# Attention features: one float32 product per head, on half of TensorE's rows each

## The chip, the cores and the metric

The kernel runs on one core of one Trainium2 chip. The metric is the device time of one execution in microseconds (us). Before the change it is 971.33 us, the median of three runs (971.07 to 971.48).

## What is computed

The input of two MLPs is an attention with random features (FAVOR). For batch 4, 8 heads, 576 tokens and head size 64, with `omega` of 128 x 64:

```python
def phi(x):                                   # x is q or k, scaled by 64 ** -0.25
    proj = np.einsum('bhsd,md->bhsm', x, omega)
    h = proj - np.sum(x * x, axis=-1, keepdims=True) / 2.0
    h = h - np.max(h, axis=-1, keepdims=True)
    return np.exp(h) / np.sqrt(m)
kv = einsum('bhsm,bhsd->bhmd', phi(k), v);  z = sum over s of phi(k)
out = (phi(q) @ kv) / (phi(q) . z + 1e-6)
```

The term in `x * x` is the same for all 128 features of a token, so it falls out when the maximum is taken away, and the kernel leaves it out. The result, 2304 tokens x 512, goes through two MLPs (512 to 2048 to 512), the first with a leaky ReLU whose slopes are `alpha`, the second with a clipped square. All is float32.

## The kernel before

**Attention.** Two heads make a pair: head 0 of a pair stands in partitions 0 to 63 of the q and k tile, head 1 in 64 to 127. There are 16 pairs, four for each batch. `kq` of a pair has 512 columns of k, 512 of q, and a block of 128 columns with the last 64 tokens of k and of q. `features` (line 332) forms the products of blocks of 128 tokens: the block is the stationary operand and `om` (128 x 256) the moving one. `om` holds the scaled omega twice, block-diagonal, so one product gives both heads' features, 2 x 128 columns. Two blocks fill one PSUM bank of 512 columns. VectorE takes the negated maximum of each head and token (line 351), ScalarE the exponentials, 128 columns at a time with that maximum as bias (line 354). Then follow the key sums (line 359), the transposes of the q features (line 414), the quotients (line 450) and `back` (line 473), which writes the attended tokens to `x`.

**Two ways to form a product.** Pairs 0 to 5 (`N_FULL = 6`) use plain float32 products (line 342). For the later pairs, `split_columns` (line 327) makes a float32r part `xh` on ScalarE (line 226) and a rest `xl` on GpSimd or VectorE (line 237 or 236), and `mm3` (line 241) forms the product in three float32r passes with `om_hi` and `om_lo`. The same `mm3` serves the quotients of the later pairs and both MLPs.

**MLPs.** A unit is one slice of 128 hidden features for one group of tokens. Sixteen units make a group's layer; the groups are batch 0, batch 1, batch 2, and batch 3 with the left-over tokens. Weights come as packed 64-bit words and are converted on ScalarE, VectorE and GpSimd (`convert`, line 252), then split into float32r parts `w_hi` and `w_lo` (`split_weights`, line 299).

**Order.** All instructions are put in order by a small planner (`Plan`, line 38) when the program is built. Each piece of work is a stream that asks for engines, tokens or events, and gives an estimated duration for each step. The planner takes the step that can start first; ranks break ties. TensorE's steps of attention have ranks below those of the MLPs, so they go first. On the chip each engine then runs its instructions in that fixed order. Buffers are tokens: there is one token each for the k features, the q features, the left-over features and the transposed features, and two for the q and k tiles (`xs_of_pair`).

**Banks.** PSUM has eight banks. `h0` and `h1` belong to the MLPs' hidden products. Attention may use the other six (`y0` to `y3`, `a0`, `a1`) until the first MLP unit has been projected; from then on `y0` to `y3` go to the MLPs and attention has `a0` and `a1`. `give` (line 321) hands a bank back.

Of the kernel before, what the change touches and what calls it, by code (L numbers as in the profile page):

```python
# [8 lines left out]
F32 = mybir.dt.float32  # L9
# [123 lines left out]
def _dve(n, emit, handicap=0.0):  # L133
    return "dve", 65 + 1.05 * n, emit, handicap
# [18 lines left out]
def _pe(ns, emit):  # L153
    return "pe", ns, emit
# [7 lines left out]
def favor_attention_two_mlps(  # L162
# [21 lines left out]
    P = 128  # L184
# [13 lines left out]
    AHEAD = 5  # L198
    N_FULL = 6
    WARM = 18  # L200

    const = ctx.enter_context(tc.tile_pool(name="const", bufs=1))
    wpool = ctx.enter_context(tc.tile_pool(name="w", bufs=NF))
# [10 lines left out]
    def ev(*key):  # L214
        return events.setdefault(key, Event())

    def done(*key):
        plan.set(ev(*key))

    def bank(tag):  # L220
        return psum.tile([P, 512], F32, tag=tag, name=tag)


    def hi_of(hi, src, dve=None):
        n = src.free_size()
        ops = [_act(n, lambda: nc.scalar.activation(hi, src, AF.Copy))]  # L226
        if dve is not None:
            ops.append(_dve_fast(n, lambda: nc.vector.tensor_copy(hi, src), dve))
        return ops

    def lo_of(lo, src, hi, engines=("dve",), bias=0.0):
        n = src.free_size()
        args = lo, src, hi.bitcast(F32), ALU.subtract
        ops = {
            "dve": _dve(n, lambda: nc.vector.tensor_tensor(*args), bias),  # L235
            "dve2": _dve_two(n, lambda: nc.vector.tensor_tensor(*args), bias),  # L236
            "pool": _pool(n, lambda: nc.gpsimd.tensor_tensor(*args)),  # L237
        }
        return [ops[e] for e in engines]
# [6 lines left out]
    def mm3_ns(n):  # L246
        return 3 * max(109.0, 13.5 + n / 2.4)
# [69 lines left out]
    xs_of_pair, v_slots, split_slot = Tokens([0, 1]), Tokens([0, 1]), Tokens([0])  # L317
    k_slot, q_slot, l_slot, t_slot, den_slot = (Tokens([0]) for _ in range(5))
    kv_slots = Tokens([0, 1])

    def give(tag):
        if tag[0] == "a" or not started:
# [1 line left out]
        else:  # L324
            plan.put(y_banks, tag)

    def split_columns(x, xh, xl, c, key):
        yield hi_of(xh[:, c], x[:, c], 500)
        yield lo_of(xl[:, c], x[:, c], xh[:, c], ("dve2", "pool"), 5000)
        done(*key)  # L330

    def features(pool, xf, xh, xl, t0, n, dst, key, needs):
        yield ev(*needs)
        tag = yield free_banks
        pr = bank(tag)

        def products():
            for t in range(n):
                c = slice((t0 + t) * P, (t0 + t + 1) * P)
                o = pr[:, t * 2 * M : (t + 1) * 2 * M]  # L340
                if xh is None:
                    nc.tensor.matmul(o, xf[:, c], om, start=True, stop=True)  # L342
                else:
                    mm3(o, xh[:, c], xl[:, c], om_hi, om_lo, True, True)

        yield _pe(n * (432 if xh is None else mm3_ns(2 * M)), products)
        pv = pr[:, : 2 * n * M].rearrange("p (n m) -> p n m", m=M)
        nm = pool.tile([P, 4], F32, tag="nm", name="nm", bufs=8)[:, : 2 * n]  # L350
        yield _dve(2 * n * M, lambda: nc.vector.tensor_reduce(nm, pv, AX.X, ALU.max, negate=True))  # L351
        for i in range(2 * n):
            yield _act(
                M, lambda: nc.scalar.activation(dst[:, i, :], pv[:, i, :], AF.Exp, bias=nm[:, i : i + 1]), 40  # L354
            )
        give(tag)
        done(*key)

    def key_sums(pool, kf, lf, vm, vl, pair):
        for key in ("k0", "k1", "l"):  # L360
# [52 lines left out]

    def transposed(qf, lf, qh, ql, h, pair):
        if h < 2:
            yield ev("q0", pair)
            yield ev("q1", pair)
        else:
            yield ev("l", pair)
        tag = yield free_banks  # L420
        ft = bank(tag)

        def products():
            if h < 2:
                for j in range(NJ):
                    nc.tensor.transpose(ft[:, j * P : (j + 1) * P], qf[:, 2 * j + h, :], ident)
            else:
                nc.tensor.transpose(ft[:, :P], lf[:, 1, :], ident)

        yield _pe(109 * (NJ if h < 2 else 1), products)  # L430
        done("qt", pair, h)
        if h < 2:
            src, hi, lo = ft, qh[:, h, :SM], ql[:, h, :SM]
        else:
            src = ft[:, :P].rearrange("m (h t) -> m h t", h=2)
            hi, lo = qh[:, :, SM:], ql[:, :, SM:]
        if pair < N_FULL:
            hi = hi.bitcast(F32)
            n = src.free_size()
            yield [  # L440
                _act(n, lambda: nc.scalar.activation(hi, src, AF.Copy)),
                _dve(n, lambda: nc.vector.tensor_copy(hi, src), 300),
            ]
        else:
            yield hi_of(hi, src)
            yield lo_of(lo, src, hi)
        give(tag)
        done("qs", pair, h)
# [90 lines left out]
    def attend(pool):  # L539
        for pair in range(B * NP):  # L540
            b, hp = divmod(pair, NP)
            r = (3 + b, b - 7)
            yield ev("kq", pair, -1 if pair == 0 else 0)
            yield split_slot
            xt, vm, vl = loaded.pop(pair)
            one = pair < N_FULL
            xh = xl = None
            if not one:
                xh = pool.tile([P, 2 * SM + P], F32R, tag="xh", name="xh")
                xl = pool.tile([P, 2 * SM + P], F32R, tag="xl", name="xl")  # L550
            pieces = [slice(0, SM), slice(2 * SM, 2 * SM + P), slice(SM, 2 * SM)]
            for c, key in zip(pieces, ("xk", "xl", "xq")):
                if one:
                    plan.add(passed(("kq", pair, -1 if key == "xk" and pair == 0 else 0), (key, pair)), *r)
                else:
                    plan.add(split_columns(xt, xh, xl, c, (key, pair)), *r)
            yield k_slot
            kf = pool.tile([P, NJ * 2, M], F32, tag="kf", name="kf")
            plan.add(features(pool, xt, xh, xl, 0, 2, kf[:, :4], ("k0", pair), ("xk", pair)), *r)
            plan.add(features(pool, xt, xh, xl, 2, 2, kf[:, 4:], ("k1", pair), ("xk", pair)), *r)  # L560
            yield l_slot
            lf = pool.tile([P, 2, M], F32, tag="lf", name="lf")
            plan.add(features(pool, xt, xh, xl, 2 * NJ, 1, lf, ("l", pair), ("xl", pair)), *r)
            yield q_slot
            qf = pool.tile([P, NJ * 2, M], F32, tag="qf", name="qf")
            plan.add(features(pool, xt, xh, xl, NJ, 2, qf[:, :4], ("q0", pair), ("xq", pair)), *r)
            plan.add(features(pool, xt, xh, xl, NJ + 2, 2, qf[:, 4:], ("q1", pair), ("xq", pair)), *r)
            plan.add(reload(pool, pair, ("k0", "k1", "l", "q0", "q1") if one else ("xk", "xl", "xq")), *r)
            yield ev("v", pair)
            plan.add(key_sums(pool, kf, lf, vm, vl, pair), *r)  # L570
            yield t_slot
            qh = pool.tile([M, 2, S], F32R, tag="qh", name="qh")
            ql = pool.tile([M, 2, S], F32R, tag="ql", name="ql")
            for h in range(3):
                plan.add(transposed(qf, lf, qh, ql, h, pair), *r)
            plan.add(back(pool, qh, ql, b, hp, pair), *r)
            plan.add(hand_back(pair), *r)
            for key in ("k0", "k1", "l", "q0", "q1"):
                yield ev(key, pair)
            plan.put(split_slot, 0)  # L580

    def reload(pool, pair, keys):
# [2 lines left out]
        plan.put(xs_of_pair, 0)  # L585
        if pair + 2 < B * NP:
            yield from load_pair(pool, pair + 2)

    def passed(key, to):
        yield ev(*key)  # L590
        done(*to)

    def hand_back(pair):
        yield ev("qt", pair, 2)
# [196 lines left out]
    ident = const.tile([P, P], F32, name="ident")  # L791
    alpha_sb = const.tile([P, NF], F32, name="alpha_sb")
    half = const.tile([P, 1], F32, name="half")
    om_hi = const.tile([P, 2 * M], F32R, name="om_hi")
    om_lo = const.tile([P, 2 * M], F32R, name="om_lo")

    ctx.enter_context(tc.manual_schedule())
    att = ExitStack()
# [2 lines left out]
    om = pool.tile([P, 2 * M], F32, name="om")  # L801
    nc.vector.memset(om, 0.0)
    nc.vector.memset(half, 0.5)
    nc.vector.memset(om_lo.bitcast(F32), 0.0)

    warm = const.tile([P, 1], F32, name="warm")
    nc.scalar.activation(warm, half, AF.Exp)
    w = bank("h0")
    for i in range(WARM):
        nc.tensor.matmul(w[:, : 2 * M], om_lo[:, :M], om_lo, start=i == 0, stop=i == WARM - 1)  # L810
    for i in range(2):
        nc.scalar.dma_start(om[i * D : (i + 1) * D, i * M : (i + 1) * M], omega)
    vts = []
# [23 lines left out]
    def constants():  # L837
        make_identity(nc, ident)
        nc.scalar.activation(om, om, AF.Copy, scale=QK_SCALE)
        nc.scalar.activation(om_hi, om, AF.Copy)  # L840
        nc.vector.tensor_tensor(om_lo, om, om_hi.bitcast(F32), ALU.subtract)

    def setup():
        yield "act", 500, constants

    plan.add(setup(), 0)
    plan.add(load(alpha_sb, alpha, ("alpha",)), 0)
# [60 lines left out]
```

## Time and profile before

| | |
|---|---|
| median of the runs | 971.33 us |
| profiled execution, its own time | 974.34 us |
| its span | 972.5 us |
| TensorE products busy | 944.9 us |
| VectorE, ScalarE, GpSimd busy | 566.4, 530.7, 480.6 us |
| mean granted TensorE clock | 0.99 |
| first MLP product starts | 59.5 us |
| last attention x is written | about 300 us |

The profile is of one execution, and its span is the time from its first to its last instruction. PE is TensorE's products, PEld its weight loads, DVE is VectorE, ACT is ScalarE, POOL is GpSimd, SP the engine that issues most DMAs. Groups are named out<-in by the program's tiles. The end of a TensorE record is modelled, and records overlap, so the distance between two starts is the better measure of what one costs. The granted clock is 1.00 at 2.4 GHz and 0.50 at 1.2 GHz.

### The profile page before, as it was taken

The page shows a single profiled execution, that of the slowest core. Times are in us where ns is not written, and L with a number is a line of the kernel's source. Part 1 is how long each engine was busy: PE and PEld are TensorE (multiplying, and loading weights), DVE is VectorE, ACT ScalarE, POOL GpSimd, SP SyncE. Part 2 cuts the span into 40 slices and gives each one's busy share as a digit, 9 for nine tenths or more (in the row PEclk, how much of TensorE's full clock was granted, in tenths as well). Part 3 has the DMA queues.
Part 4 walks back from the last instruction along what each step waited for, and adds up shares of the span by engine and source line. Part 5 has one row for each costly group of instructions (what it writes and reads, how often), then busy time and mean ns, then how long its engine had stood idle before and what let it go on. Part 6 is the DMA issues. An engine that isn't in the chain of part 4 may idle for free.

```text
span 972.5 us, 13293 instructions
## 1 busy us (share of the span) xinstructions
PE 944.9 (97%) x4742; PEld 795.9 (82%) x4742; DVE 566.4 (58%) x949; ACT 530.7 (55%) x1131; POOL 480.6 (49%) x403
## 2 busy tenths in 40 slices
PE   8999989899999999999999999999999999999997
PEld 7877877778888888888888888888887888888886
DVE  4898778678666786556763443354336333534442
ACT  6978777677665565345442354455445444544443
POOL 0545766576445868546663334444443444333320
PEclk9999999799999999999999999999999999999999
DMA  6544444331200322202310000001001000100002
GB/s 181 151 141 136 126 133 142 107 120 38 78 1 2 107 75 99 65 1 87 130 66 1 1 1 1 0 1 44 1 1 43 1 1 1 44 1 1 1 1 65
DMA packets 33858, 53.35 MB, mean 55 GB/s; under 512 B 20993, under 2 KB 21121, under 8 KB 33793
## 3 DMA queue, kind: packets, MB, share of 16 engines
q1 hardware_dynamic: 33632, 52.45, 17.1%
q8 instruction: 37, 0.61, 0.3%
q14 instruction: 29, 0.23, 0.1%
q10 hardware_dynamic: 160, 0.07, 0.0%
HBM read 47.78 MB, written 4.72 MB: 54 GB/s over the span
## 4 chain that ended last, share of the span: by engine, by line
PE 86%; DVE 8%; ACT 3%; issue 1%; POOL 1%; DMA 1%; ACTq 0%; POOLq 0%; DVEq 0%
PE h L244 13%; PE h L242 13%; PE h L243 13%; PE y L244 11%; PE y L242 11%; PE y L243 11%; PE a L242 3%; PE a L244 3%; PE a L243 3%; PE a L377 2%; PE y L342 1%; DVE x_lo L236 1%; ACT kf L354 1%; DVE den L465 1%; DVE nm L351 1%
## 5 line engine op out<-in xcount | busy, mean ns | idle before, releaser
L237 POOL TENSOR_TENSOR w_lo<-w,w_hi 128x512 fp32r<-128x512 f32 x256 | 334.1, 1307 | 381.7 <-ACT w_hi L226 375.0
L226 ACT ACTIVATE w_hi<-w 128x512 fp32r<-128x512 f32 x256 | 161.3, 632 | 220.3 <-PE h L243 155.0
L242 PE MATMUL h<-x_hi,w_hi 128*128 128x512 f32 (+1 forms) x640 | 239.5, 374 | 1.4 <-ACT w_hi L226 1.3
L244 PE MATMUL h<-x_hi,w_lo 128*128 128x512 f32 (+1 forms) x640 | 237.4, 371 | 1.6 <-POOL w_lo L237 1.6
L243 PE MATMUL h<-x_lo,w_hi 128*128 128x512 f32 (+1 forms) x640 | 236.9, 370 | 0.0
L244 PEld LDWEIGHTS h<-x_hi,w_lo 128*128 128x128 f32 x640 | 121.2, 189 | 23.5 <-POOL w_lo L237 2.9
L242 PEld LDWEIGHTS h<-x_hi,w_hi 128*128 128x128 f32 x640 | 121.6, 190 | 21.4 <-ACT w_hi L226 1.5
L243 PEld LDWEIGHTS h<-x_lo,w_hi 128*128 128x128 f32 x640 | 121.5, 190 | 19.1
L226 ACT ACTIVATE g_hi<-h 128x512 fp32r<-128x512 f32 (+1 forms) x160 | 88.7, 554 | 85.7 <-DVE h L656 46.7
L235 DVE TENSOR_TENSOR g_lo<-h,g_hi 128x512 fp32r<-128x512 f32 (+1 forms) x160 | 100.3, 635 | 53.1 <-ACT g_hi L226 50.4
L654 DVE TENSOR_SCALAR t<-h 128x512 f32<-128x512 f32 x80 | 51.0, 638 | 135.4 <-PE h L244 133.7
L269 POOL TENSOR_TENSOR w<-w,raw 128x512 uint32<-128x512 uint32 x64 | 86.2, 1348 | 48.3 <-DVE w L268 26.0
L242 PE MATMUL y<-g_hi,w_hi 128*128 128x512 f32 x256 | 101.3, 396 | 1.2 <-ACT kf L354 1.2
L244 PE MATMUL y<-w_hi,g_lo 128*128 128x512 f32 x256 | 100.2, 391 | 2.3 <-DVE g_lo L235 2.3
L243 PE MATMUL y<-g_lo,w_hi 128*128 128x512 f32 x256 | 100.2, 391 | 0.3 <-DVE g_lo L235 0.3
L650 DVE TENSOR_SCALAR t<-h,alpha_sb 128x512 f32<-128x512 f32 x80 | 55.6, 695 | 76.5 <-PE h L244 74.9
L242 PE MATMUL y<-w_hi,g_hi 128*128 128x512 f32 x256 | 100.1, 391 | 0.0
L243 PE MATMUL y<-w_lo,g_hi 128*128 128x512 f32 x256 | 100.0, 391 | 0.0
L244 PE MATMUL y<-g_hi,w_lo 128*128 128x512 f32 x256 | 100.0, 390 | 0.0
L655 ACT ACTIVATE t<-t,half 128x512 f32<-128x512 f32 x80 | 54.4, 680 | 62.4 <-DVE t L654 62.4
L656 DVE TENSOR_TENSOR h<-h,t 128x512 f32<-128x512 f32 x80 | 51.5, 644 | 49.7 <-ACT t L655 49.7
L272 DVE SCALAR_TENSOR_TENSOR w<-raw,w 128x512 uint32<-128x512 uint32 x64 | 55.8, 887 | 14.6 <-POOL w L269 14.5
(129 smaller groups left out, 1442.3 us busy)
## 6 DMA issues: line engine op xcount, KB each, us to landing
raw<-w SPq DMA_DIRECT2D x64, 512.0 KB, 3.9
kq<-kq SPq DMA_DIRECT2D x15, 576.0 KB, 3.8
vm<-v SPq DMA_DIRECT2D x16, 256.0 KB, 3.2
out<-x SPq DMA_DIRECT2D x16, 256.0 KB, 2.0
vl<-v SPq DMA_DIRECT2D x32, 16.0 KB, 2.9
out<-x SPq DMA_DIRECT2D x4, 128.0 KB, 2.3
kq<-kq SPq DMA_DIRECT2D x1, 320.0 KB, 3.3
kq<-kq SPq DMA_DIRECT2D x1, 256.0 KB, 2.9
```

The costliest lines, as they stand in the source:

```text
L226: ops = [_act(n, lambda: nc.scalar.activation(hi, src, AF.Copy))]
L235: "dve": _dve(n, lambda: nc.vector.tensor_tensor(*args), bias),
L237: "pool": _pool(n, lambda: nc.gpsimd.tensor_tensor(*args)),
L242: nc.tensor.matmul(out_, wh, mh, start=first, stop=False)
L243: nc.tensor.matmul(out_, wh, ml, start=False, stop=False)
L244: nc.tensor.matmul(out_, wl, mh, start=False, stop=last)
L269: yield _pool(n, lambda: nc.gpsimd.tensor_tensor(d, d, low, ALU.add))
L272: lambda: nc.vector.scalar_tensor_tensor(d, e, 0x80000000, d, ALU.bitwise_and, ALU.bitwise_or),
L650: yield _dve(n, lambda: nc.vector.tensor_scalar(tn, hn, 0.0, a, ALU.min, ALU.mult))
L654: yield _dve(n, lambda: nc.vector.tensor_scalar(tn, hn, -1.0, 1.0, ALU.max, ALU.min))
L655: yield _act(n, lambda: nc.scalar.activation(tn, tn, AF.Square, bias=half[:, 0:1], scale=0.5), 50)
L656: yield _dve(n, lambda: nc.vector.tensor_tensor(hn, hn, tn, ALU.max))
```

## The change

All 16 pairs now form the features of their 512 k and 512 q tokens in the same way. For each block of 128 tokens and each head there is one float32 product of 64 rows: the block's 64 partitions of that head, times the head's 64 x 128 piece of `om`. The products of head 0 go to one bank and those of head 1 to another, four blocks of 128 columns in each, and the exponentials of each head are a stream of their own. `features` takes both banks before it starts, and the new token `two_banks` lets only one `features` gather banks at a time. The block of left-over tokens keeps a full product of 128 rows, in float32 for all pairs. The float32r parts of q, k and omega are gone, with `split_columns` and `passed`. The transposes of a head wait for that head's features. The q and k tile of every pair is handed back when its features are done. Setup's planned duration falls from 500 to 300 ns, and the warm-up products use a zeroed tile of their own.

```diff
+    ROWS_NS = 264
+    two_banks = Tokens([0])
-    def split_columns(x, xh, xl, c, key):
-        yield hi_of(xh[:, c], x[:, c], 500)
-        yield lo_of(xl[:, c], x[:, c], xh[:, c], ("dve2", "pool"), 5000)
-        done(*key)
-    def features(pool, xf, xh, xl, t0, n, dst, key, needs):
...
+    def exponentials(pool, pr, tag, dst, key):
+        n = dst.shape[1]
+        pv = pr[:, : n * M].rearrange("p (n m) -> p n m", m=M)
+        nm = pool.tile([P, 4], F32, tag="nm", name="nm", bufs=8)[:, :n]
+        yield _dve(n * M, lambda: nc.vector.tensor_reduce(nm, pv, AX.X, ALU.max, negate=True))
+        for i in range(n):
+            yield _act(
+                M, lambda: nc.scalar.activation(dst[:, i, :], pv[:, i, :], AF.Exp, bias=nm[:, i : i + 1]), 40
+            )
         give(tag)
         done(*key)
+    def features(pool, x, t0, f, keys, needs, r):
+        yield ev(*needs)
+        yield two_banks
+        tags = []
+        for h in range(2):
+            tags.append((yield free_banks))
+        plan.put(two_banks, 0)
+        prs = [bank(tag) for tag in tags]
+        def products():
+            for t in range(NJ):
+                c = slice((t0 + t) * P, (t0 + t + 1) * P)
+                for h in range(2):
+                    rows = slice(h * D, (h + 1) * D)
+                    o = prs[h][:, t * M : (t + 1) * M]
+                    nc.tensor.matmul(o, x[rows, c], om[rows, h * M : (h + 1) * M], start=True, stop=True)
+        yield _pe(NJ * ROWS_NS, products)
+        for h in range(2):
+            plan.add(exponentials(pool, prs[h], tags[h], f[:, h::2, :], keys[h]), *r)
+    def last_features(pool, x, lf, key, needs):
+        yield ev(*needs)
+        tag = yield free_banks
+        pr = bank(tag)
+        o = pr[:, : 2 * M]
+        yield _pe(
+            432, lambda: nc.tensor.matmul(o, x[:, 2 * NJ * P : 2 * NJ * P + P], om, start=True, stop=True)
+        )
+        yield from exponentials(pool, pr, tag, lf, key)
...
     def transposed(qf, lf, qh, ql, h, pair):
         if h < 2:
-            yield ev("q0", pair)
-            yield ev("q1", pair)
+            yield ev(f"q{h}", pair)
...
-            plan.add(features(pool, xt, xh, xl, 0, 2, kf[:, :4], ("k0", pair), ("xk", pair)), *r)
-            plan.add(features(pool, xt, xh, xl, 2, 2, kf[:, 4:], ("k1", pair), ("xk", pair)), *r)
+            plan.add(features(pool, xt, 0, kf, keys, ("kq", pair, -1 if pair == 0 else 0), r), *r)
...
-            plan.add(reload(pool, pair, ("k0", "k1", "l", "q0", "q1") if one else ("xk", "xl", "xq")), *r)
+            plan.add(reload(pool, pair, ("k0", "k1", "l", "q0", "q1")), *r)
...
     def constants():
         make_identity(nc, ident)
         nc.scalar.activation(om, om, AF.Copy, scale=QK_SCALE)
-        nc.scalar.activation(om_hi, om, AF.Copy)
-        nc.vector.tensor_tensor(om_lo, om, om_hi.bitcast(F32), ALU.subtract)
     def setup():
-        yield "act", 500, constants
+        yield "act", 300, constants
```

## Rows read from the trace of the kernel before

**Rows 1.** The page: busy time, share of the span and instructions of each engine.

```profile
span 972.5 us, 13293 instructions
PE 944.9 (97%) x4742; PEld 795.9 (82%) x4742; DVE 566.4 (58%) x949; ACT 530.7 (55%) x1131; POOL 480.6 (49%) x403
```

**Rows 2.** The page: the chain that ended last, shares of the span by engine.

```profile
PE 86%; DVE 8%; ACT 3%; issue 1%; POOL 1%; DMA 1%; ACTq 0%; POOLq 0%; DVEq 0%
```

**Rows 3.** Stages: stretch, its length, each engine's busy time (records), clock, DMA share, GB/s.

```profile
20.00:59.50 39.50, 36.82 (x214) 30.87 (x212) 35.08 (x67) 37.11 (x117) 18.34 (x17) 1.00 0.54 158
59.50:110.00 50.50, 47.59 (x280) 39.90 (x279) 45.09 (x87) 38.02 (x111) 29.63 (x27) 1.00 0.38 116
110.00:239.00 129.00, 116.99 (x633) 97.10 (x632) 100.33 (x186) 94.02 (x233) 86.30 (x73) 0.95 0.37 117
239.00:300.00 61.00, 61.00 (x353) 52.59 (x352) 39.46 (x78) 37.44 (x103) 28.38 (x26) 1.00 0.10 32
```

**Rows 4.** TensorE's waits, 59.5 to 239 us: total us, times, longest us.

```profile
PE a L242 <- ACT kf L354: 2.8, 3, 2.0
PE h L244 <- POOL w_lo L237: 1.6, 3, 0.7
PE a L242 <- ACT lf L354: 1.4, 1, 1.4
PE h L242 <- ACT w_hi L226: 1.3, 1, 1.3
```

**Rows 5.** Stages of 6 us, columns as in rows 3.

```profile
176.00:182.00 6.00, 2.92 (x13) 2.43 (x13) 4.27 (x9) 3.20 (x10) 4.36 (x4) 0.67 0.49 174
182.00:188.00 6.00, 5.92 (x21) 5.34 (x22) 2.31 (x4) 4.09 (x11) 3.36 (x4) 0.50 0.41 132
```

**Rows 6.** TensorE in order of time, first stage: start us, us, instruction, records.

```profile
13.07 1.90 PE L377 MATMUL y<-vm,kf 128*128 128x65 f32 x16
14.80 1.04 PE L426 MATMUL y<-ident,qf 128*128 128x128 f32 x8
...
17.84 1.89 PE L342 MATMUL y<-om,kq 128*128 128x256 f32 x8
19.57 0.65 PE L456 MATMUL y<-qh,kv_hi 128*128 128x288 f32 x2
```

**Rows 7.** Groups by line: records, busy us, mean ns, idle before and releaser.

```profile
L237 POOL TENSOR_TENSOR xl<-kq,xh 128x512 fp32r<-128x512 f32 x20 | 26.0, 1300 | 11.6 <-ACT xh L226 11.6
L342 PE MATMUL y<-om,kq 128*128 128x256 f32 x82 | 21.5, 410 | 0.9 <-ACT om L839 0.9
L226 ACT ACTIVATE xh<-kq 128x512 fp32r<-128x512 f32 x20 | 12.5, 624 | 0.0
L342 PE MATMUL a<-om,kq 128*128 128x256 f32 x26 | 6.9, 379 | 0.0
L237 POOL TENSOR_TENSOR xl<-kq,xh 128x128 fp32r<-128x128 f32 x10 | 5.2, 523 | 0.3 <-ACT xh L226 0.3
L226 ACT ACTIVATE xh<-kq 128x128 fp32r<-128x128 f32 x10 | 3.0, 302 | 0.0
```

**Rows 8.** TensorE in order of time: two MLP passes, then feature passes.

```profile
68.23 0.40 PE L243 MATMUL h<-x_lo,w_hi 128*128 128x512 f32 x1
68.47 0.40 PE L244 MATMUL h<-x_hi,w_lo 128*128 128x512 f32 x1
...
68.83 0.28 PE L243 MATMUL y<-om_lo,xh 128*128 128x256 f32 x1
68.95 0.29 PE L244 MATMUL y<-om_hi,xl 128*128 128x256 f32 x1
```

**Rows 9.** TensorE in order of time: one product behind float32 key sums, one behind float32r.

```profile
91.62 0.38 PE L242 MATMUL a<-qh,kv_hi 128*128 128x288 f32 x1
...
94.15 0.30 PE L242 MATMUL a<-qh,kv_hi 128*128 128x288 f32 x1
```

**Rows 10.** TensorE in order of time: a feature product that waited for its bank.

```profile
182.08 0.58 PE L242 MATMUL a<-om_hi,xh 128*128 128x256 f32 x1 [1.96 <-ACT kf L354]
```

**Rows 11.** DMA issues: records, KB each, median us from issue to landing.

```profile
kq<-kq SPq DMA_DIRECT2D x15, 576.0 KB, 3.8
```

More of the change, by code (lines that the diff above doesn't have):

```diff
@@ L325, in give @@
             plan.put(y_banks, tag)
-    def split_columns(x, xh, xl, c, key):
-        yield hi_of(xh[:, c], x[:, c], 500)
-        yield lo_of(xl[:, c], x[:, c], xh[:, c], ("dve2", "pool"), 5000)
-        done(*key)
-    def features(pool, xf, xh, xl, t0, n, dst, key, needs):
[L333 to L352, printed above, removed]
+    def exponentials(pool, pr, tag, dst, key):
[4 more added lines that the diff above has]
+        for i in range(n):
             yield _act(
@@ L545, in attend @@
             xt, vm, vl = loaded.pop(pair)
[L546 to L556, printed above, removed]
+            kq_in = ("kq", pair, 0)
             yield k_slot
             kf = pool.tile([P, NJ * 2, M], F32, tag="kf", name="kf")
-            plan.add(features(pool, xt, xh, xl, 0, 2, kf[:, :4], ("k0", pair), ("xk", pair)), *r)
-            plan.add(features(pool, xt, xh, xl, 2, 2, kf[:, 4:], ("k1", pair), ("xk", pair)), *r)
+            keys = ("k0", pair), ("k1", pair)
+            plan.add(features(pool, xt, 0, kf, keys, ("kq", pair, -1 if pair == 0 else 0), r), *r)
             yield l_slot
             lf = pool.tile([P, 2, M], F32, tag="lf", name="lf")
-            plan.add(features(pool, xt, xh, xl, 2 * NJ, 1, lf, ("l", pair), ("xl", pair)), *r)
+            plan.add(last_features(pool, xt, lf, ("l", pair), kq_in), *r)
             yield q_slot
             qf = pool.tile([P, NJ * 2, M], F32, tag="qf", name="qf")
-            plan.add(features(pool, xt, xh, xl, NJ, 2, qf[:, :4], ("q0", pair), ("xq", pair)), *r)
-            plan.add(features(pool, xt, xh, xl, NJ + 2, 2, qf[:, 4:], ("q1", pair), ("xq", pair)), *r)
-            plan.add(reload(pool, pair, ("k0", "k1", "l", "q0", "q1") if one else ("xk", "xl", "xq")), *r)
+            plan.add(features(pool, xt, NJ, qf, (("q0", pair), ("q1", pair)), kq_in, r), *r)
+            plan.add(reload(pool, pair, ("k0", "k1", "l", "q0", "q1")), *r)
             yield ev("v", pair)
@@ L587, in reload @@
             yield from load_pair(pool, pair + 2)
-    def passed(key, to):
-        yield ev(*key)
-        done(*to)
     def hand_back(pair):
@@ L793, in favor_attention_two_mlps @@
     half = const.tile([P, 1], F32, name="half")
-    om_hi = const.tile([P, 2 * M], F32R, name="om_hi")
-    om_lo = const.tile([P, 2 * M], F32R, name="om_lo")
     ctx.enter_context(tc.manual_schedule())
@@ L803, in favor_attention_two_mlps @@
     nc.vector.memset(half, 0.5)
-    nc.vector.memset(om_lo.bitcast(F32), 0.0)
     warm = const.tile([P, 1], F32, name="warm")
     nc.scalar.activation(warm, half, AF.Exp)
+    warm_w = const.tile([P, 2 * M], F32R, name="warm_w")
+    nc.vector.memset(warm_w.bitcast(F32), 0.0)
     w = bank("h0")
     for i in range(WARM):
-        nc.tensor.matmul(w[:, : 2 * M], om_lo[:, :M], om_lo, start=i == 0, stop=i == WARM - 1)
+        nc.tensor.matmul(w[:, : 2 * M], warm_w[:, :M], warm_w, start=i == 0, stop=i == WARM - 1)
     for i in range(2):
```

## The prediction

> **What bounds the kernel now.** I read the busy times first [rows 1]: TensorE is busy for 97% of the span and no other engine for more than 58%. The chain of work that ended last agrees: 86% of it is TensorE [rows 2]. So an instruction taken off TensorE is worth its own duration, wherever TensorE is the engine that the others wait for. Whether it is has to be read stage by stage [rows 3]. From 20 to 59.5 us, before the first MLP product, only attention runs, and two engines are full: TensorE 36.8 and ScalarE 37.1 of 39.5 us. From 59.5 to 239 us attention and the first MLP group share TensorE; it fills 94% of the part up to 110 us and 91% of the rest, and no other engine is over 90%. From 239 to 300 us TensorE is full, and after 300 us no attention is left, so the change touches nothing there. The waits of TensorE between 59.5 and 239 us are short ones: a product for a PSUM bank that ScalarE empties, and an MLP product for a weight part [rows 4]. One such wait has a second price: from 176 to 188 us the mean granted clock is 0.67 and then 0.50, the 1.2 GHz level in place of 2.4, after TensorE had been busy for only 2.9 of 6 us; the two rows together give up about 5 us [rows 5].
>
> **The change, part by part.** The unit is one block of 128 tokens of one pair: k and q have four blocks each, and one shared block holds the left-over tokens. A pair has 8 + 1 blocks, 16 pairs have 128 + 16.
>
> *What a block costs before.* In pairs 0 to 5 a float32 product leaves two records; eight records take from 17.84 to 19.57 us, 216 ns each, so a block costs 432 ns [rows 6]. That makes 54 products and 108 records, which the groups show [rows 7]. In pairs 6 to 15 a block is three float32r passes that start 0.12 us apart, 360 ns [rows 8].
>
> *What a block costs after.* Two products of half the rows and half the columns leave four records. By proportion, a record of 128 columns streams in 216 / 2 = 108 ns. A weight load is no faster: the 65-column products of the key sums, with little to stream, still take 1.73 us for 16 records, 108 ns each [rows 6]. No row of before shows two products on different row halves, so there are two ends. If both halves stream and load side by side, a block takes 2 x 108 = 216 ns. If one record follows the other, it takes 4 x 108 = 432 ns, which is today's price. I take the side-by-side end with a start cost on each record: the 256-column float32r pass takes 120 ns, 12 ns over the 108 of one load [rows 6, 8], and 216 + 4 x 12 = 264 ns. The plan's new constant says the same number, which I don't count as evidence.
>
> The Trainium skill (TensorE: Matmul & The Clock Gate, "Measured speedup vs the span model") gives 3.07 times for four row tiles. Scaled to two tiles that is 1.53 times, an estimate of 282 ns for a block, and the sum below would be 9.4 us in place of 11.3.
>
> *Pairs 0 to 5.* 48 blocks x (432 - 264) = 8.1 us less TensorE work, nearly all of it before 59.5 us. There ScalarE is as full as TensorE: it has 39.5 - 37.1 = 2.4 us of free time from 20 us on [rows 3], and the exponentials stay as they are. Some of ScalarE's work in the stage (weight conversions, exponentials of pairs 4 and 5) can give way. The ends are 0 and 8.1; I take half, 4.0 us. ScalarE is what is late next.
>
> *Pairs 6 to 15.* 80 blocks x (360 - 264) = 7.7 us less. The left-over block stays at full height and is float32 now: 10 x (432 - 360) = 0.7 us more. Net 7.0 us, beside MLP work that fills TensorE at once, so I count all of it.
>
> *Kinds of product side by side.* The features of pairs 6 to 15 were float32r amid float32r MLP products; they are float32 now. A float32r product right behind a float32 one shows 0.38 us in place of 0.30 [rows 9], 0.08 us. Three groups a pair (k, q, left-over) make 30 such changes: 2.4 us if each pays and none does already, 0 if the planner puts them beside the float32 key sums and transposes. I take 1.2 us of loss.
>
> *Splits removed.* ScalarE loses 12.5 + 3.0 = 15.5 us and GpSimd 26.0 + 5.2 = 31.2 us, all in pairs 6 to 15 [rows 7]. Neither is the bound. What it can give TensorE is its waits for weight parts, 1.6 + 1.3 = 2.9 us [rows 4], because a 1.3 us split no longer stands ahead of them in GpSimd's order. Between 0 and 2.9 I take 1.5 us of gain. A pair's k products also no longer wait for their own split; attention stays ahead of the MLP groups that use it, so I count nothing.
>
> *Two banks at once.* One group of products now asks for two banks, and two is all that attention has while the MLPs run. Behind the waiting product in TensorE's order stand MLP products, and all else waits for those. Before, five product groups of a pair each asked for one bank; after, two ask for two and one for one. The nearest row is a k product that waited 1.96 us for ScalarE's exponentials [rows 10]; such waits on kf and lf sum to 4.2 us over nine pairs before [rows 4]. The ends are 4.2 us of gain, if fewer requests mean fewer waits, and a 1.96 us wait for each of the 20 groups, 39 us of loss; by the sum in the rows I take 0.
>
> *At no cost.* The scaled omega's two float32r parts go from the start, but the first product waits for omega itself only. Each head's transposes wait for that head's features alone, which is earlier. The k and q tile is held until its features are done and not just its splits, so the load for the pair after next starts some microseconds later; it lands in 3.8 us [rows 11], against a pair's period of some 24 us (ten pairs in the 240 us after 59.5). With that cover gone it would cost up to 3.8 us a pair.
>
> *Sum.* 4.0 + 7.0 - 1.2 + 1.5 + 0 = 11.3 us. The profiled execution took 974.3 us (its span 972.5 and 1.8 around it) and becomes 963.0. The median of the runs is 971.3, 3.0 lower, so the forecast is **960.0 us**.
>
> **The rivals.**
> *R1, loads one after another (slower).* Four half-height loads of 108 ns follow each other and a block costs 432 ns. For it: the key sums show a load as a floor that no short stream gets below [rows 6], and a block doubles its loads from two to four. Against it: today's loads already run beside a stream, and the halves share no rows. Pairs 0 to 5 then gain nothing, pairs 6 to 15 lose 80 x 72 ns + 0.7 = 6.5 us, changes of kind 1.2, and the relief of 1.5 is the only gain: 6.2 us, 977.5 us. It decides once a block costs over about 370 ns, where 128 blocks give back what they save. The Trainium skill (TensorE: Matmul & The Clock Gate, "LDWEIGHTS (loading the stationary operand)") says that load time goes by columns and not by rows, which is this rival's premise; TensorEngine Tiling (Array Packing), "Key Properties", says that different tiles may load and multiply in parallel, which is against it. No row here shows either.
>
> *R2, each change between full and half height empties the array.* A 512-column record lasts 0.40 us while the next starts after 0.24 [rows 8]; if that tail of 0.16 us must run out whenever the height changes, 32 groups, in and out, cost 64 x 0.16 = 10.2 us and leave 1.1 of 11.3: 970.2 us. Nothing in the rows of before excludes it, since all its products have full height. The Trainium skill (TensorEngine Tiling, "Key Properties") says that a change of tiling mode drains TensorE, without a figure.
>
> *R3, the pair of banks brings new waits.* If ten of the 20 late k and q groups wait for 1 us longer than today, 10 us of the 11.3 go: 970.0 us; a further stretch like that at 176 us [rows 5] would make it 975.
>
> *R4, all is delivered.* Blocks at 216 ns and a ScalarE that gives way in full: 48 x 216 = 10.4, 80 x 144 - 0.7 = 10.8, relief 2.9, no loss at changes: 24.1 us, 947.2 us.
>
> **How the numbers follow.** Forecast 0.48, R1 0.13, R2 0.10, R3 0.09, R4 0.20. A measurement of this kernel can tell 0.2%, 1.9 us. Faster: the forecast, R4, and 0.08 of R2 and R3 together, 0.76. Within 0.2%: 0.08, from R2 and R3. Slower: R1 and 0.03 of R2 and R3, 0.16. The forecast's own range is 953 to 966 us (block 216 to 282 ns, first stage 1 to 8 us). The range with the rivals goes from R4's 946 to 974, which leaves R1 out.
>
> **What would show it.** Starts of four records of a block spanning about 264 ns show the block's price; 216 is R4, 432 is R1. A gap of 0.16 us before and after each group of 16 such records is R2. The first MLP product, at 59.5 us now, should come 3 to 5 us earlier, and ScalarE should be the fuller engine of that stage. Waits of TensorE for ScalarE's exponentials should stay near 4 us in sum before the first group ends; 10 us more is R3. The first MLP group should end some 11 us earlier than at about 239 us, and after 300 us the stretch up to the end should be as long as it is. A block over 370 ns, or TensorE's waits grown by more than what its products save, makes the forecast wrong.

## The result, and the profile after

The kernel after takes 954.68 us in the median (954.25 to 956.27), the kernel before 971.2. The ratio is 0.9836 with a 95% interval of 0.9819 to 0.9853: 16.5 us faster, where 11.3 was forecast. The profiled execution took 956.27 us, against 974.34 before; these two lie 18.1 us apart, so the stages below add up to more than the 16.5 us of the medians.

The page of the kernel after: span, busy times, and the chain that ended last. Its rows answer to [rows 1, 2].

```profile
span 954.4 us, 13551 instructions
PE 931.8 (98%) x4908; PEld 776.5 (81%) x4908; DVE 557.9 (58%) x944; ACT 515.8 (54%) x1102; POOL 453.6 (48%) x375
PE 88%; DVE 6%; ACT 4%; issue 1%; DMA 0%; POOL 0%; ACTq 0%; DVEq 0%; POOLq 0%
```

TensorE is still the bound. To see where the time went, the span is cut at two events: the first MLP product, and the end of the second MLP group (its last unit's copy to `x` begins). Stages of the kernel before, then of the kernel after; columns as in rows 3.

```profile
6.50:59.50 53.00, 50.26 (x278) 42.55 (x278) 41.28 (x77) 46.41 (x152) 18.99 (x18) 1.00 0.56 162
59.50:349.00 289.50, 274.25 (x1475) 229.61 (x1474) 221.09 (x401) 198.32 (x495) 178.25 (x153) 0.98 0.28 88
349.00:972.00 623.00, 616.15 (x2975) 519.79 (x2973) 303.49 (x470) 284.11 (x484) 281.74 (x219) 1.00 0.09 29
```

```profile
6.50:58.40 51.90, 45.03 (x374) 35.27 (x374) 37.84 (x78) 44.70 (x145) 18.54 (x18) 0.97 0.55 164
58.40:331.10 272.70, 266.51 (x1547) 217.54 (x1546) 205.01 (x381) 177.93 (x459) 139.44 (x117) 0.99 0.26 85
331.10:954.00 622.90, 615.91 (x2974) 519.63 (x2972) 314.47 (x484) 291.26 (x498) 294.07 (x226) 1.00 0.09 33
```

The stage before the MLPs gives 1.1 us, the middle stage 16.8, the rest nothing. In the middle stage TensorE's unfilled time falls from 289.5 - 274.25 = 15.3 us to 272.7 - 266.51 = 6.2, and the mean clock goes from 0.98 to 0.99. So about 9 us of the 16.8 are idle time that went, and some 3 to 5 us are time at the 1.2 GHz level (an estimate from the rows; part of the slow time was idle too). Before, two stretches ran at the lower clock, the one in [rows 5] and one at 134 us; after, one at 162 us is left. First the kernel before, then the kernel after:

```profile
134.00:140.00 6.00, 4.02 (x16) 3.01 (x15) 3.58 (x6) 4.80 (x14) 3.96 (x3) 0.75 0.52 170
162.00:166.20 4.20, 4.15 (x21) 3.45 (x22) 3.63 (x5) 2.76 (x7) 2.68 (x3) 0.59 0.46 162
```

Little is left for the products themselves. The waits point the same way: those that the profile lists in this part sum to 14.5 us before and 6.2 after. Besides [rows 4] the kernel before has these, and two of 0.8 and 0.7 us for exponentials.

```profile
PE a L426 <- DVE num L468: 1.3, 2, 1.0
PE y L242 <- ACT kf L354: 1.2, 1, 1.2
PE a L426 <- DVE ql L235: 1.2, 1, 1.2
PE a L428 <- DVE ql L235: 1.1, 1, 1.1
PE a L242 <- DVE ql L235: 1.1, 2, 0.9
```

TensorE's longest waits in the kernel after, 59 to 235 us; they answer to [rows 4]. Three more sum to 1.3 us.

```profile
PE a L361 <- ACT kf L339: 1.8, 1, 1.8
PE a L243 <- ACT lf L339: 1.3, 1, 1.3
PE a L373 <- DVE kv_lo L424: 1.0, 1, 1.0
PE h L245 <- POOL w_lo L238: 0.8, 1, 0.8
```

What a group of half-height products costs, amid MLP products (TensorE in order of time, kernel after). L361 is the new product; a bank is called y or a, its number left out.

```profile
183.23 0.39 PE L244 MATMUL h<-x_lo,w_hi 128*128 128x512 f32 x1
183.46 0.39 PE L245 MATMUL h<-x_hi,w_lo 128*128 128x512 f32 x1
183.78 1.16 PE L361 MATMUL a<-om,kq 64*128 64x128 f32 x16
184.87 0.50 PE L243 MATMUL y<-g_hi,w_hi 128*128 128x512 f32 x1
185.21 0.39 PE L244 MATMUL y<-g_lo,w_hi 128*128 128x512 f32 x1
```

And one group record by record, where the two banks have different names (kernel after, behind transposes).

```profile
66.81 0.37 PE L361 MATMUL y<-om,kq 64*128 64x128 f32 x1
66.81 0.37 PE L361 MATMUL a<-om,kq 64*128 64x128 f32 x1
67.02 0.27 PE L361 MATMUL y<-om,kq 64*128 64x128 f32 x1
67.03 0.27 PE L361 MATMUL a<-om,kq 64*128 64x128 f32 x1
67.13 0.27 PE L361 MATMUL y<-om,kq 64*128 64x128 f32 x1
67.14 0.27 PE L361 MATMUL a<-om,kq 64*128 64x128 f32 x1
...
67.69 0.27 PE L361 MATMUL y<-om,kq 64*128 64x128 f32 x1
67.70 0.27 PE L361 MATMUL a<-om,kq 64*128 64x128 f32 x1
67.90 0.70 PE L373 MATMUL a<-om,kq 128*128 128x256 f32 x2
```

The two heads' records start within 0.01 us of each other, and the next two 0.11 us later: the halves run fully side by side, and a block costs two steps, some 0.22 us. But the first step takes 0.21 us, the last 0.20. In the MLP rows a group lasts 183.78 to 184.87, 1.09 us. The record ahead takes 0.32 us to the next start and the one behind 0.34, where 0.23 is usual. A group costs 1.09 + 0.09 + 0.11 = 1.29 us, and a quarter of it is 322 ns a block; 8 steps of 0.112 would be 0.90. Going to half height and back thus costs 0.4 us a group.

### The profile page after: what moved, and what is told of

The parts are those of the page before. It is cut to its first block, busy times and chain, and to the rows that moved or that the text cites. A ratio compares the mean times of both kernels' runs of the same rounds, so it can differ in the third digit from the quotient of the medians.

```text
span 954.4 us, 13551 instructions
## 1 busy us (share of the span) xinstructions
PE 931.8 (98%) x4908; PEld 776.5 (81%) x4908; DVE 557.9 (58%) x944; ACT 515.8 (54%) x1102; POOL 453.6 (48%) x375
## 4 chain that ended last, share of the span: by engine, by line
PE 88%; DVE 6%; ACT 4%; issue 1%; DMA 0%; POOL 0%; ACTq 0%; DVEq 0%; POOLq 0%
PE h L243 13%; PE h L245 13%; PE h L244 13%; PE y L243 12%; PE y L245 12%; PE y L244 12%; PE a L243 2%; PE a L361 2%; PE a L245 2%; PE a L244 2%; PE a L395 2%; DVE nm L336 1%; PE a L443 1%; ACT kf L339 1%; DVE x_lo L237 1%
## 5 line engine op out<-in xcount | busy, mean ns | idle before, releaser
L273 DVE SCALAR_TENSOR_TENSOR w<-raw,w 128x512 uint32<-128x512 uint32 x64 | 59.0, 928 | 8.8 <-POOL w L270 8.7
```

Source lines behind the costliest of these rows:

```text
L273: lambda: nc.vector.scalar_tensor_tensor(d, e, 0x80000000, d, ALU.bitwise_and, ALU.bitwise_or),
```

## The experiments

Theory W: the gain is less product time on TensorE. Theory S: most of it is shorter waits and less time at 1.2 GHz, because the splits of q and k are gone from ScalarE and GpSimd. Theory O: it came with the new order that the planner made. Times are medians beside runs of the kernel before on the same chip (971.0 to 971.3 us).

**full32**: splits dropped, full-height products for all pairs, on the kernel before.

```diff
-            one = pair < N_FULL
+            one = True
             xh = xl = None
```

> The kernel before with the splits of q and k dropped and nothing else: all 16 pairs use full-height float32 blocks at 432 ns. TensorE gets 80 x 72 ns + 0.7 = 6.5 us more product work. Theory W (the gain of the change is product time alone): 971.2 + 6.5 = 977.7 us. Theory S (some 10 us of the gain are shorter waits and less time at 1.2 GHz, because ScalarE and GpSimd no longer split q and k): 977.7 - 10 = 967 to 969 us. Theory O (these 10 us came with the new order of instructions, whatever it was): anything from 966 to 985 us, with TensorE's waits from 59 to 340 us not tied to the splits.

Measured 962.88 us, ratio 0.991 (0.9889 to 0.9931). By the estimate TensorE has 6.5 us more product work, and the kernel is 8.1 us faster: dropping the splits is worth some 14.6 us. W falls. S has the direction, but its 967 to 969 us is missed by 4 us, and O's range is missed too.

**idle_splits**: the reverse, on the kernel after.

```diff
+            if pair >= N_FULL:
+                for c in (slice(0, SM), slice(2 * SM, 2 * SM + P), slice(SM, 2 * SM)):
+                    plan.add(idle_split(xt, xh, xl, c), *r)   # hi_of, lo_of as before
```

> The kernel after, with the splits of q and k of pairs 6 to 15 put back on ScalarE and GpSimd as they were; nothing reads their results. TensorE's products stay as in the kernel after. Theory S: the waits and the 1.2 GHz time come back, 963 to 966 us. Theory W: 954 to 957 us. Theory O: either, since the order changes again.

968.94 us, ratio 0.9986 (0.9968 to 1.0004): 14.3 us slower than after, with the same products, and 3 us slower than theory S said. Two experiments from either side give nearly the same price.

**idle_scalar, idle_gpsimd**: one engine's half of them each. The cut is against idle_splits; each run has one of the two new lines.

```diff
-        yield hi_of(xh[:, c], x[:, c], 500)
-        yield lo_of(xl[:, c], x[:, c], xh[:, c], ("dve2", "pool"), 5000)
+        yield hi_of(xh[:, c], x[:, c])                        # idle_scalar
+        yield lo_of(xl[:, c], x[:, c], x[:, c], ("pool",))    # idle_gpsimd
```

> The kernel after with only the ScalarE half of the splits of pairs 6 to 15 put back (15.5 us of work that nothing reads). If ScalarE's load makes the 14 us that both halves cost together: 966 to 970 us. If GpSimd's makes it: 954 to 957 us. If they share it: 959 to 963 us.

> The kernel after with only the GpSimd half of the splits of pairs 6 to 15 put back (31.2 us of work that nothing reads, without a wait for ScalarE). If GpSimd's load makes the 14 us: 966 to 970 us. If ScalarE's makes it: 954 to 957 us. If they share it: 959 to 963 us.

959.08 us (0.9858 to 0.9887) with ScalarE's half and 968.76 us (0.9953 to 0.9987) with GpSimd's. GpSimd's half alone brings all 14 us, with 25.4 us of GpSimd's time by its trace and not the 31.2 expected; ScalarE's half brings 4.4. The two don't add up.

**same_order_gpsimd**: work for GpSimd that the planner does not see.

```diff
+            if idle is not None:                              # in products(), pairs 6 to 15
+                c = slice(t0 * P, (t0 + NJ) * P)
+                nc.gpsimd.tensor_tensor(idle[:, c], x[:, c], x[:, c], ALU.subtract)
```

> The kernel after with 20 subtractions of 128 x 512 put on GpSimd, one behind each k and q group of pairs 6 to 15 (26 us, nothing reads them). The planner does not know of them, so every other instruction of every engine keeps the order of the kernel after. If GpSimd's time itself is what TensorE waits for: 962 to 969 us, as with idle_gpsimd. If idle_gpsimd was slow because the planner made another order: 954 to 957 us.

958.49 us, ratio 0.986 (0.9831 to 0.9889): 3.8 us slower than after, between the two answers. With 21.9 us of GpSimd's work back by the trace (25.4 in idle_gpsimd) and all else in its order, about a quarter of the 14 us returns; the interval overlaps that of the kernel after, so this 3.8 is rough. The other 10 us were seen only where the planner had the splits to place. In the plan a GpSimd step also keeps VectorE's `dve2` steps from starting, since both ask for `ports` (`USES` in `Plan`), so planned splits move VectorE's work too. No run takes that apart.

The order-kept part has a visible side on VectorE. Two groups of its weight conversion over the whole span, in the kernel after and then in this run:

```profile
L273 DVE SCALAR_TENSOR_TENSOR w<-raw,w 128x512 uint32<-128x512 uint32 x64 | 59.0, 928 | 8.8 <-POOL w L270 8.7
L269 DVE TENSOR_SCALAR w<-raw 128x512 uint32<-128x512 uint32 x64 | 38.1, 599 | 0.6 <-ACT raw L265 0.6
```

```profile
L273 DVE SCALAR_TENSOR_TENSOR w<-raw,w 128x512 uint32<-128x512 uint32 x64 | 61.4, 965 | 10.1 <-POOL w L270 9.8
L269 DVE TENSOR_SCALAR w<-raw 128x512 uint32<-128x512 uint32 x64 | 40.0, 629 | 0.7 <-ACT raw L265 0.7
```

Together they are busy 4.3 us longer, while the maxima that VectorE reads from PSUM (`nm`, 128 x 4 from bank a) take 683 and 682 ns. How much of the 3.8 us comes by this was not measured.

**after_latency230, before_latency230**: the same work in another order.

```diff
-    LATENCY = {"pe": 210.0, "dma": 2200.0}
+    LATENCY = {"pe": 230.0, "dma": 2200.0}
```

> The kernel after with the planner's latency behind TensorE at 230 ns in place of 210: the same instructions in another order. Theory S: 952 to 958 us, as after. Theory O (a new order alone moves the time by 10 us): outside of 948 to 962 us.

> The kernel before with the planner's latency behind TensorE at 230 ns in place of 210: the same instructions in another order. Theory S: 968 to 975 us, as before. Theory O: outside of 964 to 978 us, or as low as 958 us if the order before was an unlucky one.

955.72 us (0.9806 to 0.9865) and 967.52 us (0.9941 to 0.999): +1.0 and -3.5 us. The expectation for the second (968 to 975) missed by half a microsecond. In these two draws an order alone moves 1 and 3.5 us, and the order before was perhaps somewhat unlucky; neither draw crosses the gap.

The middle stages of these kernels, from first MLP product to end of second group (columns as in rows 3).

full32:

```profile
59.30:338.00 278.70, 273.50 (x1385) 227.94 (x1384) 217.88 (x389) 188.31 (x479) 151.12 (x123) 1.00 0.29 95
```

idle_splits:

```profile
58.30:345.40 287.10, 274.51 (x1546) 222.93 (x1545) 213.09 (x383) 190.62 (x487) 171.96 (x150) 0.97 0.25 81
```

idle_gpsimd:

```profile
58.00:342.90 284.90, 273.12 (x1546) 219.66 (x1545) 212.27 (x382) 181.38 (x463) 166.46 (x148) 0.98 0.26 82
```

idle_scalar:

```profile
57.90:331.40 273.50, 265.95 (x1545) 216.32 (x1544) 206.74 (x377) 189.20 (x483) 138.38 (x115) 1.00 0.26 85
```

same_order_gpsimd:

```profile
58.50:334.70 276.20, 268.75 (x1547) 218.50 (x1546) 210.28 (x381) 178.41 (x459) 161.22 (x137) 0.99 0.26 84
```

before_latency230:

```profile
60.30:343.80 283.50, 270.84 (x1469) 226.50 (x1468) 215.37 (x384) 195.25 (x488) 171.38 (x150) 0.99 0.27 86
```

TensorE's unfilled time is the stage's length less PE. What the clock gave up is summed over stretches of 4 us, each length times what the granted clock lacks of 1.00; the two can overlap. Both in us:

| | profiled execution | unfilled | given up by the clock |
|---|---|---|---|
| before | 974.3 | 15.3 | 6.8 |
| idle_splits | 969.1 | 12.6 | 8.5 |
| idle_gpsimd | 968.8 | 11.8 | 6.8 |
| before_latency230 | 967.5 | 12.7 | 3.4 |
| full32 | 963.7 | 5.2 | 0.0 |
| same_order_gpsimd | 959.8 | 7.5 | 3.4 |
| idle_scalar | 958.4 | 7.6 | 0.0 |
| after | 956.3 | 6.2 | 1.7 |

The price of the planned GpSimd splits is both: some 6 us of idle time and 5 to 7 us at the lower clock. Unfilled time alone does not set the clock: the reordered kernel before has 12.7 us of it and gives up 3.4.

**heads_apart**: the heads of a group one behind the other, on the kernel after.

```diff
-            for t in range(NJ):
+            for h in range(2):
...
-                for h in range(2):
+                for t in range(NJ):
```

> The kernel after, but a group's 8 products of head 0 come first and those of head 1 behind them, so that neighbours lie on the same half of the rows. If only products on different halves run side by side, a group of 16 records takes 16 x 108 = 1.73 us in place of 0.90: 0.83 x 20 groups of pairs 6 to 15 = 16.6 us in full, and 0 to 10 us for the 12 groups of the first stage, which has spare time on TensorE: 971 to 981 us. If half-height products are cheap for another reason: 954 to 957 us.

The median is 971.7 us (ratio 0.9954 to 1.0023), but nine of its ten runs lie in two clusters, around 964 and around 974 us, and the profiled run is one of the lower. There a group lasts 1.64 us, not 1.09, and not the 1.73 expected:

```profile
186.50 1.71 PE L361 MATMUL a<-om,kq 64*128 64x128 f32 x16
188.14 0.50 PE L243 MATMUL y<-g_hi,w_hi 128*128 128x512 f32 x1
```

0.55 us x 20 groups is 11 us, of which the lower cluster shows 9 (1.8 of them before the first MLP product, which starts at 60.1 us). Side by side is what makes half height cheap. The edit also puts neighbours into one bank, but a change of bank alone brings no overlap: in the kernel before, full-height records to bank a and to bank y start at 17.62 and 17.84 us, the usual 0.22 us apart. Why other runs take 10 us more is open.

**early_halves, late_halves**: half height in pairs 0 to 5 only, on the kernel before; and in pairs 6 to 15 only, on the kernel after.

```diff
+            if one:                                           # early_halves
+                plan.add(halves(pool, xt, 0, kf, (("k0", pair), ("k1", pair)), ("xk", pair), r), *r)
+            if pair < N_FULL:                                 # late_halves
+                plan.add(full_height(pool, xt, 0, kf[:, :4], keys[0], k_in), *r)
+                plan.add(full_height(pool, xt, 2, kf[:, 4:], keys[1], k_in), *r)
```

> The kernel before with half-height products in pairs 0 to 5 only; pairs 6 to 15 keep splits and three float32r passes. By the trace after, in which the first MLP product comes 1.1 us earlier, 969 to 971 us. By the prediction's 4.0 us for this part, 967 us. If the early part is where the gain was made, under 962 us.

> The kernel after with full-height blocks of 432 ns, one bank each, in pairs 0 to 5, as before the change; pairs 6 to 15 as after. If half height gains nothing before the first MLP product, as early_halves says: 953 to 956 us. If the early part gives the 1.1 us by which the first MLP product comes earlier: 955.8 us. By the prediction's 4.0 us: 958.7 us.

971.43 us (0.9992 to 1.0019) and 956.15 us (0.9826 to 0.9856). By the medians half height before the MLPs is worth between 0 and 1.5 us. The first MLP product does not come earlier by it: 60.0 us in early_halves against 59.5 in the kernel before, 58.4 in the kernel after against 57.7 in late_halves. At least 15 of the 16.5 us come from pairs 6 to 15.

**early_gpsimd**: does ScalarE bound the stage before the MLPs?

```diff
+        early = key[0] == 0 and key[1] < 4
         yield [
...
-        ]
-        yield _act(n, lambda: nc.scalar.activation(low, h, AF.Copy, scale=2.0**-13))
+        ][early:]
+        if early:
+            yield _pool_one(n, lambda: nc.gpsimd.tensor_scalar(low, h, 2.0**-13, 0.0, ALU.mult, ALU.add))
+        else:
+            yield _act(n, lambda: nc.scalar.activation(low, h, AF.Copy, scale=2.0**-13))
```

> The kernel after with the two ScalarE steps of the first four units' weight conversions moved to GpSimd, which has time there; some 7 us less ScalarE work before the first MLP product. If ScalarE bounds the stage before the MLPs, the first MLP product comes 2 to 5 us earlier than at 58.4 us and the time is 950 to 953 us. If it does not, the start stays within 1 us and the time at 954 to 956 us.

955.83 us (0.9809 to 0.9876). The stage from 20 to 57.5 us, first in the kernel after and then in this one:

```profile
20.00:57.50 37.50, 32.47 (x267) 24.97 (x267) 30.79 (x65) 34.47 (x110) 17.70 (x17) 1.00 0.49 148
```

```profile
20.00:57.50 37.50, 31.93 (x264) 24.83 (x264) 31.94 (x61) 29.02 (x100) 24.13 (x27) 1.00 0.53 163
```

ScalarE's time falls from 34.5 to 29.0 us, and the first MLP product stays at 58.4 us. ScalarE's load is not what alone holds this stage.

**quot32_all**: the float32 form of key sums and quotients in all pairs, on the kernel after.

```diff
-    N_FULL = 6
+    N_FULL = 16
```

> The kernel after with the float32 form of keys sums and quotients in all 16 pairs (N_FULL = 16): TensorE gets 40 x (486 - 396) ns = 3.6 us more, VectorE loses about 22 us of splits (kv_lo, ql). Theory S, taken to VectorE: waits fall again by more than 3.6 us, 946 to 953 us. Theory W (product time alone): 954.7 + 3.6 = 958.3 us.

953.84 us (0.9796 to 0.9829): the lowest median of all, 0.8 us under the kernel after, whose interval overlaps, and just above the range of theory S. VectorE is busy for 538.9 us in place of 557.9. The estimated 3.6 us more on TensorE are paid back, but little more than that. Its middle stage:

```profile
58.40:327.40 269.00, 265.46 (x1505) 216.00 (x1504) 191.61 (x327) 185.81 (x472) 146.90 (x123) 1.00 0.29 94
```

Unfilled time is 3.5 us, against 6.2: the reserve that relief can still give in this stage is nearly used up.

## Why the prediction was right, and where it was not

The direction and the range held; the size was 5.2 us short, and the terms were not the ones that made it. That the time lies in the range is partly luck: the products and the first stage gave 6 to 7.5 us less than forecast, and the removed splits 12.5 us more.

*The block.* The side-by-side end was the right one: the steady price is about 0.22 us, not the 264 ns taken. The start cost on every record was wrong, and in its place stands a cost per group: 0.4 us for going to half height and back. That is the cost that R2 named, which was given 0.32 us (twice 0.16) and a chance of 0.10 as an alternative; it acts beside the cheap block, not in place of it. The Trainium skill (TensorEngine Tiling (Array Packing), "Key Properties") says that different tiles may load and multiply in parallel and that a change of tiling mode drains TensorE. The trace agrees on the first, with starts 0.01 us apart; for the second it shows the 0.4 us, not what happens in them. Together a block costs 322 ns, worse than forecast.

The 0.4 us is not the change between float32r and float32. In full32 a full-height float32 group stands amid float32r products:

```profile
106.03 0.40 PE L244 MATMUL h<-x_hi,w_lo 128*128 128x512 f32 x1
106.26 1.89 PE L342 MATMUL a<-om,kq 128*128 128x256 f32 x8
107.80 0.58 PE L242 MATMUL h<-x_hi,w_hi 128*128 128x512 f32 x1
108.22 0.39 PE L243 MATMUL h<-x_lo,w_hi 128*128 128x512 f32 x1
```

From 106.03 to 108.22 are 2.19 us, which is 0.23 + 8 x 0.216 + 0.23, with nothing over. So the 1.2 us that the sum took for changes of kind is not found in this row; the prediction read it from the length of one record behind key sums. Here too the record behind the group is long, 0.58 us, but from start to start it costs nothing.

*Pairs 6 to 15, with the changes of kind.* Forecast 7.0 - 1.2 = 5.8 us. The products gave 80 x (360 - 322) = 3.0 less 0.7 for the left-over blocks, 2.3 us. From full32 to after the median falls by 8.2 us, up to 1.5 of it from pairs 0 to 5, where 80 x (432 - 322) is 8.8 us; in the middle stages TensorE's busy time falls by 273.50 - 266.51 = 7.0 us. So TensorE's product time counts nearly in full here, as assumed.

*Pairs 0 to 5.* Forecast 4.0, measured 0 to 1.5 us. The step that failed is the naming of ScalarE as the one thing that is late next: early_gpsimd takes 5.5 us off it and gains nothing. In the kernel after the chain that ended last does run over ScalarE for most of 37 to 52 us; in early_gpsimd a chain over TensorE, VectorE and ScalarE in turn is as long. TensorE stands idle for 51.9 - 45.0 = 6.9 us of the stage in place of 2.7. Which link of a pair's chain sets its pace was not settled, and the order has a part in it: in after_latency230 the first MLP product comes at 56.6 us.

*Splits removed.* This is the mis-sized term: 1.5 us forecast, 14 us measured (full32 and idle_splits). The bound of 2.9 us was read from the waits for weight parts [rows 4]. That list names the last thing that a product waited for, and the stage had 15.3 us of unfilled time and 6.8 us given up by the clock, spread over many releasers: the waits for VectorE's `ql` and `num` alone, 4.7 us, are longer than those for weight parts. The experiments split the 14 us: about 4 are GpSimd's time itself with the order kept; about 10 were seen only with the GpSimd splits in the plan. An order changed by another planned latency moved 1 and 3.5 us. What in those orders makes TensorE wait is open: no single repeated wait carries it. The waits for `ql` and `num` on VectorE fit in part: 0.3 us after, 0.6 in same_order_gpsimd, 2.2 in idle_gpsimd, 4.8 in idle_splits, but also 2.7 in idle_scalar, which is 10 us faster than idle_gpsimd.

*Two banks at once.* No loss came, as taken. TensorE's waits for exponentials fell from 6.9 us (the prediction's 4.2 left out those on y banks) to 3.7, one of them 1.8 us of a feature group for its bank. In full32, with one bank for a group and no splits, they are 2.0 us; no run has the two banks as its only difference. R3 did not occur.

*R1* is refuted by the records that start 0.01 us apart. *R4* was near on the steady block (0.22 us for its 216 ns), wrong on the first stage and on the changes, and its relief of 2.9 us was as far below the 14 as the forecast's.

*The signs on what follows.* From the end of the second MLP group on the two kernels take 623.0 and 622.9 us, so nothing changed there. But the sign on the first group missed: its first copy to `x` starts at 209.6 us in place of 238.9, 29 us earlier and not 11, and the last attention x starts at 322.0 us in place of 304.5. The new plan puts the first group ahead and attention later, which the prediction did not foresee; so its stretch "after 300 us" is not the same work in both kernels.

## What to carry to other kernels

Products on separate row halves run side by side and halve the steady price of a block, but each trip to half height costs a fixed time, 0.4 us here; make the groups long and price the group, not the record. When work leaves an engine that is not the bound, take the bound's whole unfilled and slow-clock time in that stage as the most it can return (here 15.3 + 6.8 us, of which some 14 came back), and not the waits that name that engine (2.9 us). In a kernel ordered by a planner, part of that return comes only by way of a new plan: put the work back both in and outside the plan to tell the two apart.

## What the runs showed of the hardware

With the heads apart, a group of 16 half-height records took 1.64 us, shorter than 16 steps of 0.108: even then the second head's first records ran while the first head's last were under way. In the group at 68.31 us the second head's first record starts at 68.86, the first head's last at 69.19. A full-height float32 group amid float32r products cost nothing beyond its own 8 x 0.216 us; a half-height group cost 0.4 us more than its steps. And 21.9 us of GpSimd's subtractions, whose results nothing reads, came with two groups of VectorE's steps at 965 and 629 ns in place of 928 and 599 and cost some 3.8 us by the medians, in an otherwise unchanged order.
